# Eight subtractions moved from VectorE to GpSimd, and a small indirect transfer ahead of the first gathers, in a routed expert kernel

## The chip, the cores and the metric

The kernel runs on one core of one Trainium2 chip. The metric is device microseconds of one execution. Traces are of one profiled execution; times in them count from its first instruction. Engines are named as in the profile: PE is TensorE's matmuls and PEld its weight loads, DVE is VectorE, ACT is ScalarE, POOL is GpSimd, SP is SyncE.

## The reference

Windowed attention with a linear bias makes the tokens of a mixture of experts. Each expert takes exactly 4608 / 8 = 576 tokens, given out greedily by descending score.

```python
# attention: batch 8, heads 8, sequence 576, head size 64, window 128
scores = where(mask, q @ k.T / 8 + bias, -1e9)
x = (softmax(scores) @ v)            # -> tokens [4608, 512]

# experts: N, D, E, F = 4608, 512, 8, 1024
cap = N // E
logits = x @ w_gate
for idx in argsort(-logits.flatten()):      # greedy, each token once, each expert at most cap
    tok, e = idx // E, idx % E
    if assigned[tok] < 0 and counts[e] < cap:
        assigned[tok] = e; counts[e] += 1
for e in range(E):
    mask = assigned == e
    out[mask] = maximum(x[mask] @ w1[e], 0) @ w2[e]
```

All inputs and outputs are float32.

## The kernel before

**Two parts.** `attention` runs first (to about 203 us); it stores the tokens to `x`, a tensor in device memory, with DMAs on SP's queue. Then `Router.start` finds the tokens of the first expert (`phase(0)`, VectorE with small matmuls), and `layer_moe` does the experts one by one. The route of expert k+1 and k+2 (`phase`, a generator that is advanced from `slot`) is worked out by VectorE while TensorE multiplies for expert k.

**Exactness by two parts.** The matmuls take fp32r operands, so each operand is split into a high part (the value rounded to fp32r) and a low part (what is left). `MoE.split` does so for weights: from a raw float32 chunk of 128x1024 ScalarE makes the high part (line 896), and VectorE subtracts it from the raw chunk to get the low part, in two halves of 512 columns (line 898). Both lie in one tile `hl`. The raw tiles have 4 buffers (`raw`), the split ones 10 (`wt`). An expert has four chunks for its first layer and four for its second.

**An expert.** `gather` issues five indirect DMAs on POOL's queue (line 907), which fetch the expert's tokens by the indices `idx`. `turn` transposes them on TensorE and splits them into `xh` and `xl` (lines 931 to 935). `layer1` multiplies (line 954), ScalarE makes the high part of the result `hh` (line 960), VectorE the low one `hlo` (line 965). `layer2` multiplies high by high, high by low weights, low by high (lines 983, 984, 986), and the result goes out by an indirect DMA on POOL's queue (line 995). For expert 0 `layer1` does the first 256 tokens for all columns before the rest, and the last two of its five transposes come later.

**What sets the order.** Tiles and semaphores are laid out by a planner that runs through the program with a cost for each instruction and writes out a fixed order for each engine; an instruction that comes earlier in the program has priority when several are ready in the plan. `keep_in_program_order` and `issue_after` hold some instructions to the program's order. On the chip, each engine goes through its list in that order, and one that waits holds up all behind it on its engine. Where loads and splits stand in the program is set by two lists, of which each entry is expert (relative to k), layer, chunk and earliest slot:

```python
W_SPLIT = [(0, 1, 0, 2), (0, 1, 1, 6), (0, 1, 2, 10), (0, 1, 3, 14),
           (1, 0, 0, 17), (1, 0, 1, 20), (1, 0, 2, 23), (1, 0, 3, 26)]
```

The first four are the second layer of the current expert, the others the first layer of the next. The first layer of expert 0 is split in `layer_moe` itself.

**The route's steps on VectorE, and what waits for them.** For an expert after the first, `few` picks 16 candidates per partition (lines 791 to 807: `q`, `qt`, `few`, `fy`, `fq`, `fa`, `OHf`), then three times a key (`kf`, line 817), an indicator (`ind`, line 565) and a count on TensorE (`m`, line 589). After that come `T` (695), the chosen expert's number `ei` (710), `m` (713), a running sum `run` (715), `ex` (717) with a matmul (720), and the indices `idx` (756). POOL does three instructions of this (lines 768, 773, 774), of 128x288 float32. The weights of an expert are loaded by SP only when its number `ei` is there (`loads`, lines 886 and 889). For expert 0 the route's instructions stand under line 456.

Of the kernel before, what the change touches and what calls it, by code (L numbers as in the profile page):

```python
# [5 lines left out]
F32 = mybir.dt.float32  # L6
F32R = mybir.dt.float32r
BF = mybir.dt.bfloat16
I32 = mybir.dt.int32
AF = mybir.ActivationFunctionType  # L10
ALU = mybir.AluOpType
# [4 lines left out]
E, DM, F, N = 8, 512, 1024, 4608  # L16
# [861 lines left out]
class MoE:  # L878
# [10 lines left out]
            nc.sync.dma_start(raw, (self.w1d, self.w2d)[layer][bass.ds(v, 1), c].rearrange("o p f -> (o p) f"))  # L889
            yield raw  # L890

    def split(self, raw):

        nc = self.nc
        hl = self.p["wt"].tile([128, 2, 1024], F32R, name="hl")
        self.last = nc.scalar.copy(hl[:, 0, :], raw)  # L896
        for c in (0, 512):
            nc.vector.tensor_tensor(hl[:, 1, c:c + 512], raw[:, c:c + 512], hl[:, 0, c:c + 512].bitcast(F32), ALU.subtract)  # L898
        return hl

    def gather(self, idx):
        nc = self.nc
        gs = []
        for h in range(5):
            r = 128 if h < 4 else 64
            g = self.p["g"].tile([128, DM], F32, name="g")
            nc.gpsimd.indirect_dma_start(out=g[:r, :], out_offset=None, in_=self.x,  # L907
                                         in_offset=bass.IndirectOffsetOnAxis(ap=idx[:r, h:h + 1], axis=0))
            gs.append((g, r))
        return gs  # L910
# [134 lines left out]

def layer_moe(tc, P, C, r, x, w1, w2, out, exact):
    m = MoE(tc, P, C, x, w1, w2, out)
    g = m.gather(r.idx[0])
    raw = list(m.loads(r.ei[0], 0, range(SOON)))
    route = (n for k in range(1, E) for n in r.phase(k, exact))  # L1050
    with tc.issue_after(r.last.ins):
        for _ in range(EARLY0):
            next(route)
    W = {(0, 0): [m.split(raw[c]) for c in range(HI0)]}
    with tc.issue_after(r.last_pe.ins):
        m.idle = P["ps_h"].tile([128, 512], F32, name="ph")
        m.keep_warm(WARM0)
    tn = m.turn(g, True)
    with tc.issue_after(m.last.ins):
        next(tn)  # L1060

    with tc.issue_after(m.turned.ins):
        late = P["rt"].tile([1, 1], I32, name="late")
        last = tc.nc.vector.tensor_copy(late, r.ei[0][0:1, 0:1])
    raw += list(m.loads(late, 0, range(SOON, 4)))
    with tc.issue_after(m.last.ins):
        for _ in range(TURN0 - 1):
            next(tn)
    W[0, 0] += [m.split(raw[c]) for c in range(HI0, 4)]
    with tc.issue_after(last.ins):  # L1070
        for _ in range(EARLY - EARLY0):
            next(route)
    for _ in tn:
        pass
    st = dict(wait=0, turn=0)
    raws, loaders = {}, {}

    def slot(k, i):

        st["wait"] -= 1  # L1080
        if st["wait"] <= 0 and (k + 1 not in r.idx or k + 2 not in r.idx and i >= AHEAD[min(k, 2)]):
            st["wait"] = next(route, 0)
        for e, layer, c, due in W_LOAD:
            e += k
            if i >= due and e in r.ei and len(raws.get((e, layer), ())) == c:
                if c == 0:
                    loaders[e, layer] = m.loads(r.ei[e], layer)
                    raws[e, layer], W[e, layer] = [], []
                raws[e, layer].append(next(loaders[e, layer]))
                break  # L1090
        for e, layer, c, due in W_SPLIT:
            e += k
            if i >= due and len(W.get((e, layer), (0,) * 9)) == c and len(raws[e, layer]) > c:
                W[e, layer].append(m.split(raws[e, layer][c]))
                break
        if i >= 16 and k + 1 in r.idx:
            if k not in gathers:
                gathers[k], st["turn"] = m.turn(m.gather(r.idx[k + 1])), i + TURN_WAIT
            elif i >= st["turn"]:
                next(gathers[k], None)  # L1100
                st["turn"] = i + TURN_STEP

    gathers = {}
    for k in range(E):
        i = 0
        for _ in m.layer1(W.pop((k, 0)), m.xg, k == 0):
            slot(k, i)
            i += 1
        for _ in range(9):
            if len(W.get((k, 1), ())) < 4:  # L1110
                slot(k, i - 1)
        for _ in m.layer2(W.pop((k, 1)), m.h, r.idx[k], k == E - 1):
            slot(k, i)
            i += 1
        if k == E - 2:

            with tc.issue_after(m.sent.ins):
                m.nc.gpsimd.drain()
        if k < E - 1:
            while k + 1 not in r.idx:  # L1120
                next(route)
            while len(W.get((k + 1, 0), ())) < 4:
                slot(k, 31)
            if k not in gathers:
                gathers[k] = m.turn(m.gather(r.idx[k + 1]))
            for _ in gathers[k]:
                pass
# [12 lines left out]
def moe_attn_kernel(tc, qk, v, w1, w2, wn, rel, ident, cst, out):  # L1140
    nc = tc.nc
    with ExitStack() as es:
# [25 lines left out]
        for k, b in (("ps_g", 1), ("ps_h", 4), ("ps_o", 2)):  # L1168
            P[k] = es.enter_context(tc.tile_pool(name=k, bufs=b, space=PSUM))
        layer_moe(tc, P, C, r, x, w1, w2, out, False)  # L1170
        again = P["rs"].tile([1, 1], I32, name="again")
        nc.vector.tensor_copy(again, r.flag[0:1, 0:1])
        go = nc.values_load(again[0:1, 0:1], min_val=0, max_val=1)
        with tc.If(go > 0):
            r.start(True)
            layer_moe(tc, P, C, r, x, w1, w2, out, True)
# [26 lines left out]
```

## Time and profile before

| | |
|---|---|
| median of 3 runs | 692.58 us (692.04 to 695.5) |
| the profiled execution | 692.76 us, its span 691.0 us |
| mean granted TensorE clock | 0.983 |
| PE busy | 660.8 us (96%) |
| DVE busy | 453.4 us (66%) |
| ACT busy | 325.1 us (47%) |
| POOL busy | 152.4 us (22%) |
| low parts of weights on DVE (line 898) | 128 instructions, 682 ns each |
| gathers on POOL (line 907) | 40 instructions, 1086 ns each |

The span is from the first to the last instruction of the profiled execution; the execution's own time has a little around it. Busy time is the union of an engine's instructions; on POOL it is rough. In the order of time a row gives start and duration in us, engine, line, operation, output and inputs, shapes, count, and in brackets how long the engine stood idle before and what ended it.

### The profile page before, as it was taken

Reading aid. Unit: us, or ns where it says so; the run is one execution under the profiler, and the core shown is the slowest. Engines: PE = TensorE matmul, PEld = TensorE weight load, DVE = VectorE, ACT = ScalarE, POOL = GpSimd, SP = SyncE. Lnnn points to the kernel's source line nnn. Section 1 sums busy time; section 2 is a strip of 40 time slices with the busy share of each in tenths; the row PEclk is TensorE's granted clock in tenths of the full one; section 3 lists DMA queues with packets and bytes.
Section 4 is the critical chain, followed back from the end, with each engine's and each line's share of the span. In section 5 each row is a group of like instructions: output and inputs, shape, how many; then the busy total and the mean of one; then the engine's idle time right before and its main releaser. Section 6 shows DMA issues by size and latency. Waiting matters only on the chain.

```text
span 691.0 us, 18850 instructions
## 1 busy us (share of the span) xinstructions
PE 660.8 (96%) x7266; PEld 581.2 (84%) x7267; DVE 453.4 (66%) x1876; ACT 325.1 (47%) x991; POOL 152.4 (22%) x337
## 2 busy tenths in 40 slices
PE   8999999999973999899999999999999999999996
PEld 5899889989872788689789889889988988988986
DVE  6678888887877889699578738818846524523210
ACT  6898899898861434333243233224214324323211
POOL 4122222222120204113250231131132022011011
PEclk9999999999995999999999999999999999999999
DMA  8466665757332707335263245135135325301001
GB/s 313 139 205 206 195 227 173 219 179 223 109 90 80 228 25 251 121 131 191 74 206 102 93 132 158 45 123 183 55 114 172 104 92 152 110 30 39 1 25 49
DMA packets 35138, 92.71 MB, mean 134 GB/s; under 512 B 3808, under 2 KB 13152, under 8 KB 35040
## 3 DMA queue, kind: packets, MB, share of 16 engines
q1 hardware_dynamic: 29152, 72.55, 32.4%
q0 software_dynamic: 5888, 18.88, 8.4%
q8 instruction: 59, 0.97, 0.6%
q14 instruction: 39, 0.32, 0.2%
HBM read 72.54 MB, written 18.87 MB: 132 GB/s over the span
## 4 chain that ended last, share of the span: by engine, by line
PE 85%; DVE 7%; DMA 4%; ACT 2%; issue 1%; SPq 0%; POOL 0%; POOLq 0%; DVEq 0%
PE ph L954 26%; PE po L983 10%; PE po L984 10%; PE po L986 8%; PE s L53 7%; PE x L53 7%; PE pt L53 7%; PE pt L160 6%; PE pg L931 2%; DMA raw<-in_w_dram 2%; DVE hl L898 1%; ACT hl L896 1%; ACT u L147 1%; PE m L589 1%; DMA rel_sb<-in_rel_dram 1%
## 5 line engine op out<-in xcount | busy, mean ns | idle before, releaser
L954 PE MATMUL ph<-xh,hl 128*128 128x288 f32 (+2 forms) x1024 | 189.8, 299 | 0.0
L954 PEld LDWEIGHTS ph<-xh,hl 128*128 128x128 f32 x1024 | 154.3, 189 | 1.0
L983 PE MATMUL po<-hl,hh 128*128 128x512 f32 (+1 forms) x328 | 130.8, 399 | 0.0
L147 ACT ACTIVATE u<-u,mn 128x192 f32<-128x192 f32 (+2 forms) x288 | 124.0, 438 | 5.5 <-DVE mn L137 5.5
L984 PE MATMUL po<-hl,hh 128*128 128x512 f32 (+1 forms) x328 | 126.5, 386 | 0.0
L954 PE MATMUL ph<-xl,hl 128*128 128x288 f32 (+2 forms) x512 | 115.7, 298 | 0.0
L960 ACT ACTIVATE hh<-ph 128x288 fp32r<-128x288 f32 (+2 forms) x128 | 46.8, 408 | 144.6 <-PE ph L954 144.3
L986 PE MATMUL po<-hl,hlo 128*128 128x512 f32 (+1 forms) x264 | 102.1, 387 | 0.0
L898 DVE TENSOR_TENSOR hl<-raw,hl 128x512 fp32r<-128x512 f32 x128 | 84.9, 682 | 13.7 <-ACT hl L896 13.2
L137 DVE CUSTOM_DVE_ANT_0 u<-s,bm 128x192 f32<-128x192 f32 (+1 forms) x248 | 71.8, 346 | 32.4 <-PE s L53 31.7
L995 POOL DMA_INDIRECT out_dram<-o,idx x40 | 44.6, 1116 | 204.2 <-ACT o L990 125.0
L954 PEld LDWEIGHTS ph<-xl,hl 128*128 128x128 f32 x512 | 84.1, 189 | 0.1
L935 DVE TENSOR_TENSOR xl<-pg,xh 128x512 fp32r<-128x512 f32 (+1 forms) x37 | 23.7, 640 | 83.0 <-ACT xh L934 82.9
L965 DVE SCALAR_TENSOR_TENSOR hlo<-ph,hh 128x288 fp32r<-128x288 f32 (+2 forms) x128 | 49.8, 417 | 39.7 <-ACT hh L960 39.5
L896 ACT CAST hl<-raw 128x1024 fp32r<-128x1024 f32 x64 | 65.5, 1049 | 17.1 <-DMA raw<-in_w_dram 12.1
L983 PEld LDWEIGHTS po<-hl,hh 128*128 128x128 f32 x328 | 61.8, 188 | 11.1
L984 PEld LDWEIGHTS po<-hl,hh 128*128 128x128 f32 x328 | 61.9, 189 | 10.6
L990 ACT COPY o<-po 128x512 f32<-128x512 f32 (+1 forms) x33 | 18.9, 573 | 95.5 <-PE po L986 60.5
L907 POOL DMA_INDIRECT g<-x,idx x40 | 43.4, 1086 | 83.4 <-PE pg L931 33.8
L53 PE MATMUL s<-qk 64*64 64x192 f32 (+1 forms) x992 | 60.5, 327 | 0.6 <-DMA qk<-in_qk_dram 0.3
L986 PEld LDWEIGHTS po<-hl,hlo 128*128 128x128 f32 x264 | 49.6, 188 | 10.1
L147 ACT ACTIVATION_READ_ACCUMULATOR u<-u,mn 128x1 f32 x288 | 55.8, 194 | 0.0
(236 smaller groups left out, 939.2 us busy)
## 6 DMA issues: line engine op xcount, KB each, us to landing
raw<-in_w_dram SPq DMA_DIRECT2D x64, 512.0 KB, 4.3
qk<-in_qk_dram SPq DMA_DIRECT2D x32, 576.0 KB, 5.1
v<-in_v_dram SPq DMA_DIRECT2D x32, 288.0 KB, 3.8
x<-xb SPq DMA_DIRECT2D x14, 512.0 KB, 3.7
x<-xb SPq DMA_DIRECT2D x8, 128.0 KB, 3.4
x<-xb SPq DMA_DIRECT2D x4, 256.0 KB, 2.5
g<-x,idx POOLq DMA_INDIRECT x40, 3.4
out_dram<-o,idx POOLq DMA_INDIRECT x40, 2.8
```

The lines of the kernel that those rows point to most:

```text
L53: put(nc.tensor.matmul(out, w, a, start=start, stop=stop, skip_group_check=True))
L137: put(nc.vector.tensor_tensor_reduce(out=weights(n, t, h), in0=x[:, c:c + 64 * m].rearrange("q (j k) -> q j k", k=64), in1=bm[n % NP][:, y ...
L147: put(nc.scalar.activation(u, u, AF.Exp, bias=st["mn"][:, i:i + 1], scale=-1.0, accum_out=st["sm"][:, i:i + 1]))
L896: self.last = nc.scalar.copy(hl[:, 0, :], raw)
L898: nc.vector.tensor_tensor(hl[:, 1, c:c + 512], raw[:, c:c + 512], hl[:, 0, c:c + 512].bitcast(F32), ALU.subtract)
L954: nc.tensor.matmul(pp[t], w[:, a, j, fo:fo + 128], x[:, j, cut[t]:cut[t + 1]], start=(j == 0 and a == 0 and x is xh), stop=(j == 3 and a = ...
L960: nc.scalar.activation(o, pp[t], AF.Relu)
L965: nc.vector.scalar_tensor_tensor(d, pp[t][:, c0:c1], 0.0, o[:, c0:c1].bitcast(F32), ALU.max, ALU.subtract)
L983: nc.tensor.matmul(out, a, wh, start=(f == 0), stop=False)
L984: nc.tensor.matmul(out, a, wl, start=False, stop=(f == 7 and t == 4))
L986: nc.tensor.matmul(out, hl[:, f, 128 * t:128 * t + 128], wh, start=False, stop=(f == 7))
L995: self.sent = nc.gpsimd.indirect_dma_start(out=self.out, out_offset=bass.IndirectOffsetOnAxis(ap=idx[:r, t:t + 1], axis=0), in_=o[:r, :], ...
```

## The change

Two things are done.

`rehearse` is called at the start of `layer_moe`, before the first `gather`. On POOL it sets 16 indices to zero and issues one indirect DMA that fetches row 0 of `x` 16 times into 16 partitions of a tile of the output pool `o` (3 buffers); nothing reads it. As a read of `x` it waits for the stores of `x`.

`split` takes an engine for the subtraction. In `slot` that is GpSimd where the expert's number is 0. The only entries with that number are those of expert 0's second layer (the first four of `W_SPLIT` at k = 0): four chunks, two halves each, eight instructions of 128x512. All other splits stay on VectorE.

```diff
-    def split(self, raw):
+    def split(self, raw, eng=None):
 
         nc = self.nc
         hl = self.p["wt"].tile([128, 2, 1024], F32R, name="hl")
         self.last = nc.scalar.copy(hl[:, 0, :], raw)
         for c in (0, 512):
-            nc.vector.tensor_tensor(hl[:, 1, c:c + 512], raw[:, c:c + 512], hl[:, 0, c:c + 512].bitcast(F32), ALU.subtract)
+            (eng or nc.vector).tensor_tensor(hl[:, 1, c:c + 512], raw[:, c:c + 512], hl[:, 0, c:c + 512].bitcast(F32), ALU.subtract)
         return hl
+
+    def rehearse(self):
+
+        nc = self.nc
+        row = self.p["rt"].tile([16, 1], I32, name="row", bufs=1)
+        nc.gpsimd.memset(row, 0)
+        got = self.p["o"].tile([128, DM], F32, name="o")
+        nc.gpsimd.indirect_dma_start(out=got[:16, :], out_offset=None, in_=self.x,
+                                     in_offset=bass.IndirectOffsetOnAxis(ap=row[:, 0:1], axis=0))
...
     m = MoE(tc, P, C, x, w1, w2, out)
+    m.rehearse()
     g = m.gather(r.idx[0])
...
             if i >= due and len(W.get((e, layer), (0,) * 9)) == c and len(raws[e, layer]) > c:
-                W[e, layer].append(m.split(raws[e, layer][c]))
+                W[e, layer].append(m.split(raws[e, layer][c], None if e else m.nc.gpsimd))
                 break
```

## The prediction

> **What bounds the kernel now.** I read the page first, then the granted clock and busy time by stage, then TensorE's waits, and only then the order of time around each wait.
>
> ```profile
> span 691.0 us, 18850 instructions
> PE   8999999999973999899999999999999999999996
> ```
> ```profile
> 231.00:243.00 12.00, 12.00 (x101) 11.85 (x98) 10.43 (x41) 7.40 (x12) 0.00 (x0) 1.00 0.83 278
> 243.00:246.00 3.00, 1.63 (x20) 1.20 (x19) 2.13 (x7) 2.04 (x5) 0.00 (x0) 1.00 0.07 27
> 246.00:260.00 14.00, 13.87 (x98) 12.34 (x98) 12.21 (x56) 2.74 (x7) 1.91 (x3) 1.00 0.01 2
> 260.00:295.00 35.00, 32.91 (x200) 26.58 (x200) 27.29 (x97) 14.18 (x20) 10.36 (x9) 1.00 0.53 184
> 295.00:303.00 8.00, 7.10 (x54) 6.61 (x51) 7.13 (x32) 1.42 (x4) 3.15 (x4) 1.00 0.08 19
> ```
> ```profile
> PE m L589 <- DVE ind L565: 3.1, 2, 1.8
> PE m L720 <- DVE ex L717: 1.4, 2, 1.0
> PE pg L931 <- DMA g<-x,idx: 0.8, 1, 0.8
> ```
>
> The first fence is the page: TensorE is full in nearly every slice. The second is busy time by stage (columns after the length: PE, weight load, DVE, ACT, POOL, clock, DMA share, GB/s). The third is TensorE's waits from 222 us to the end. From there on it waits 3.1 + 1.4 + 0.8 = 5.3 us in all, five times, the last of them in the stage that ends at 303. So whatever this change can give without removing matmuls is at most 5.3 us. Four waits are for VectorE's routing of the next experts; one is for the first gather. The clock is full in all these stages, so it is not in the sum.
>
> The change's stage is 231 to 303 us. VectorE is busy 12.21 of 14 us from 246 to 260: while TensorE starts expert 0, VectorE both routes expert 1 and makes low parts.
>
> **Part 1, the small transfer ahead of the gathers.** It adds on POOL's queue one memset and one indirect DMA of 16 rows, both before the five gathers, and takes one buffer of the output tile, not used before expert 0's second layer.
>
> ```profile
> 206.53 0.47 SPq L273 DMA_DIRECT2D x<-xb  x1
> L907 POOLq EVENT_SEMAPHORE  x30: 17/17/14065, 206.4 to 565.0; - x30
> 222.73 0.33 DVE L456 SCALAR_TENSOR_TENSOR idx<-ia 64x5 int32<-64x5 f32 x2
> 224.03 1.18 POOL L907 DMA_INDIRECT g<-x,idx  x1 [22.18 <-DVE L L456]
> 225.52 1.13 POOL L907 DMA_INDIRECT g<-x,idx  x1 [0.30 <-issue]
> 227.59 0.66 PE L931 MATMUL pg<-ident_sb,g 128*128 128x128 f32 x4 [0.79 <-DMA g<-x,idx]
> 266.27 0.32 DVE L756 SCALAR_TENSOR_TENSOR idx<-ia 64x5 int32<-64x5 f32 x2
> 267.33 1.04 POOL L907 DMA_INDIRECT g<-x,idx  x1 [7.39 <-issue]
> ```
>
> Its own cost lies in a hole: it must wait for the last store of x (issued at 206.53 on SP, which it does not pass), and POOL's queue stands in one wait of 14.07 us until the indices come. A gather's issue takes 1.18 us, so the cover is some ten times what is put in it; without that cover it would cost its 1.2 us ahead of the gathers.
>
> What it can give: the first indices end at 223.06 and the first gather starts at 224.03, 0.97 us later. Against the second gather, which follows the first by 0.30, up to 0.67 of that could be a cold first issue. But expert 1's gather, no longer the first, starts 267.33 - 266.59 = 0.74 us after its indices. That is the nearest row (same form, same wait), so I take 0.97 - 0.74 = 0.2 us, with ends 0 and 0.67. Below nothing is excluded by the 14 us hole. TensorE's wait for this gather is 0.79 us, so no more than that could be had.
>
> **Part 2, eight subtractions from VectorE to POOL.** Four weight chunks of expert 0's second layer, two halves each (first row, with least, median and greatest ns, and first and last start):
>
> ```profile
> L898 DVE TENSOR_TENSOR hl<-raw,hl x8: 676/680/686, 240.0 to 249.4; 128x512 fp32r<-128x512 f32 x8
> L774 POOL TENSOR_TENSOR L<-Lt,L 128x288 f32<-128x288 f32 x6 | 5.1, 850 | 0.5
> L299 POOL TENSOR_TENSOR by<-Lp 128x160 f32<-128x160 f32 x7 | 3.7, 524 | 0.6
> 238.16 1.05 ACT L896 CAST hl<-raw 128x1024 fp32r<-128x1024 f32 x1
> 257.22 0.43 POOL L773 TENSOR_SCALAR Lt<-T 128x288 f32<-128x288 bf16 x1 [26.55 <-DVE T L695]
> 259.03 0.14 DVE L710 TENSOR_SCALAR ei<-ef 128x1 int32<-128x1 f32 x1
> 246.18 0.39 PE L984 MATMUL po<-hl,hh 128*128 128x512 f32 x1
> 246.41 0.39 PE L986 MATMUL po<-hl,hlo 128*128 128x512 f32 x1
> 264.12 0.40 PE L984 MATMUL po<-hl,hh 128*128 128x512 f32 x1
> ```
>
> VectorE loses 8 x 0.68 = 5.4 us. POOL's price is an estimate from its own two subtraction-like rows: (850 - 524) / (288 - 160) = 2.55 ns per column, so 850 + 224 x 2.55 = 1.42 us for 512 columns, 11.4 us for eight. POOL is idle 26.55 us before 257.22, so it has room. The first cast ends at 239.21, so uninterrupted POOL would be done near 251. Two things must hold to call this free on TensorE. The first low part used (246.18) needs only chunk 0, ready near 242. The next one is used at 264.12; its cover is 13 us. And the raw buffers, which POOL frees up to 2 us later than VectorE did, are next loaded for expert 1, whose number comes at 259.03. Without these covers the price would be POOL's lateness one for one.
>
> Now what VectorE's relief is worth at each TensorE wait. First the wait of 1.37 us:
>
> ```profile
> 239.98 0.68 DVE L898 TENSOR_TENSOR hl<-raw,hl 128x512 fp32r<-128x512 f32 x1
> 240.69 0.68 DVE L898 TENSOR_TENSOR hl<-raw,hl 128x512 fp32r<-128x512 f32 x1
> 241.28 0.17 DVE L802 TENSOR_SCALAR fy<-few 128x16 f32<-128x16 f32 x1
> 242.10 0.17 DVE L805 SCALAR_TENSOR_TENSOR fa<-fq,few 128x16 bf16<-128x16 f32 x1
> 242.26 0.69 DVE L898 TENSOR_TENSOR hl<-raw,hl 128x512 fp32r<-128x512 f32 x1
> 242.86 0.22 DVE L807 TENSOR_TENSOR OHf<-c_eb,fa 128x128 bf16<-128x128 bf16 x1
> 243.90 0.68 DVE L565 TENSOR_TENSOR ind<-kf,c_i 128x1024 bf16<-128x1024 bf16 x1
> 244.63 0.42 PE L589 MATMUL m<-OHf,ind 128*128 128x16 bf16 x8 [1.37 <-DVE ind L565]
> ```
>
> Three of the eight stand ahead of `ind` in VectorE's order, each holding back the next instruction by 0.60 (240.69 to 241.28, for one): 1.8 us, more than the wait. So the upper end is all 1.37. The lower end is set by what happens when POOL and VectorE read at once:
>
> ```profile
> L713 DVE SCALAR_TENSOR_TENSOR m<-am,kmx,sel x7: 236/561/564, 258.5 to 530.6; 128x36 bf16<-128x36 bf16 x7
> L715 DVE TENSOR_TENSOR_SCAN run<-c_ones,m x7: 215/851/859, 259.4 to 531.1; 128x36 bf16<-128x36 bf16 x7
> 258.54 0.56 DVE L713 SCALAR_TENSOR_TENSOR m<-am,kmx,sel 128x36 bf16<-128x36 bf16 x1
> 258.39 0.67 POOL L768 TENSOR_TENSOR L<-L,pen 128x288 f32<-128x288 f32 x1 [0.74 <-DVE ov L776]
> ```
>
> `m` takes 0.24 us alone and 0.56 as a rule; here it ends at 259.10, just after POOL's subtraction ends at 259.06. `run` takes 0.22 alone and 0.85 as a rule. So a VectorE instruction with two inputs in SBUF stands until POOL's running one is done: 0.32 and 0.64 us, 50 to 75% of a POOL instruction. [...]
>
> Ahead of the wait there are three such: `fa`, `OHf` and `ind`. If POOL runs its 1.42 us instructions back to back from 239.21, they end near 240.65, 242.1, 243.5; each of the three VectorE instructions slips in after one of them, `ind` starts near 243.6 to 244.0, and 0 to 0.3 of the 1.37 is won. The measured rows are nearer to that end than to a free run, but only if POOL is always ahead, so I take 0.4, ends -0.1 and 1.37.
>
> The second long wait, 1.78 us:
>
> ```profile
> 282.23 0.42 PE L589 MATMUL m<-OHf,ind 128*128 128x16 bf16 x8 [1.78 <-DVE ind L565]
> ```
>
> It is the first count of expert 2's routing, and stands behind expert 1's. After `ind` at 243.90 five of the eight are left (they end by 250), 5 x 0.60 = 3.0 us off VectorE's queue, less one more `ind` that may meet POOL (at most 1.42). So expert 1's routing can run some 1.6 to 3.0 us earlier, as far as TensorE's count matmuls, which stand between layer matmuls at places the planner chose, move with it. Those places are not seen here. Ends 0 and 1.78; I take 0.7, under half, since both the planner and expert 1's weight transfers stand between. The two waits for `ex` (1.4 together) come from `m` and `run` meeting POOL's older instructions, which stay: 0.1, ends 0 and 1.4.
>
> **Sum.** 0.2 + 0.4 + 0.7 + 0.1 = 1.4 us. The profiled execution took 692.76 us (span 691.0 and 1.76 around it), so 691.4 by it, with a span of 689.6. The median of the runs is 692.58, 0.18 below; from there 691.2, which is my number.
>
> **Rivals.**
> (a) All of VectorE's waits go: POOL's subtractions fall mostly between VectorE's two-input instructions, and the planner moves the counts forward. Then 0.67 + 1.37 + 1.78 + 1.4 = 5.2 us: 687.4. For it: VectorE is the only thing these waits name. Against it: `m` and `run` met POOL in nearly all of seven executions.
> (b) The exclusion eats it: the 4 two-input instructions from 240 to 251 (`fa`, `OHf`, two `ind`) each stand a whole 1.42, 5.7 us, against 8 x 0.60 = 4.8 won. VectorE gains nothing or loses 0.9, and the time is 692.6 to 693.5, no change. For it: the same seven rows. Against it: a full wait each time needs the worst phase.
> (c) Slower: TensorE comes to wait for POOL. No POOL row writes fp32r, the type of the low part, so 1.42 us is from another output type. In the order seen, each of the eight may take (264.12 - 239.21) / 8 = 3.1 us before anything waits; that is the point from which it decides. At three times my price, 4.26 us, POOL ends at 239.21 + 34.1 = 273.3, while the last low part is wanted about 18 matmuls of 0.23 us (246.18 to 246.41) after 264.12, at 268.3. TensorE stands 5.0 us there, and the time is 692.58 + 5.0 - 0.2 = 697.4. Against it: VectorE's 0.68 us for this form is no more than 512 columns cost it with another type (`ind`, 1024 columns of bf16, 0.68), so the type need not matter. Fillers such as the matmul at 246.18, drawn forward onto a low part not yet made, would cost less.
> (d) The small transfer does nothing: then 0.2 is missing, inside the range; it is part of every case.
>
> **How the numbers follow.** Partial gain as summed 0.46, (a) 0.22, (b) 0.22, (c) 0.10. Within 0.5% (3.46 us, about what a measurement of this kernel can tell from no change) lie the forecast and (b): 0.68. (a) is faster and (c) slower by over that. The range runs from (a), 687.4, to 694.5, 1.0 beyond (b)'s 693.5 for fillers that wait a little on POOL; the forecast's own part of it is 689.1 to 692.6.
>
> **What would show it.** Expert 0's eight POOL subtractions near 1.4 us each, back to back from 239 to 252. `ind` before 243.9, and TensorE's first wait for it well below 1.37; that at 282 below 1.78. `fa`, `OHf` or `ind` longer than 0.17, 0.22 and 0.68 would show the exclusion. The first gather 0.74 us after its indices, not 0.97. Wrong would be: TensorE waiting for a low part on POOL, a POOL price far from 1.42, or a layer order so changed that new waits appear after 303.

## The result and the profile after

The changed kernel takes 700.56 us (median of 6 runs, 699.31 to 700.98) against 692.31 us before (6 runs beside it): slower, ratio 1.011 with a 95% interval of 1.0089 to 1.0131. The prediction was 691.2 us, in a range of 687.4 to 694.5, with 0.10 for slower. It was wrong in sign and far outside its range.

The page of the changed kernel, span and two rows of the 40 slices (PE busy, granted TensorE clock):

```profile
span 698.7 us, 18859 instructions
PE   8999999999965799899999999999999999999995
PEclk9999999999985979999999999999999999999999
```

The fourteenth slice of TensorE (227 to 244.5 us) has gone from 9 to 7, and in the fifteenth the clock row has a 7. (The 6 and 5 ahead of it are the route of expert 0, which was there before; the slices are wider now.) TensorE's waits from 222 us on (us in total, times, longest):

```profile
PE m L589 <- DVE ind L565: 7.0, 2, 5.4
PE m L720 <- DVE ex L717: 1.4, 2, 0.9
PE pg L940 <- DVE xl L944: 0.9, 1, 0.9
```

Three of the five waits of before are as they were: the second one for `ind` is 1.56 us (1.78), the two for `ex` are 0.43 and 0.94 (0.44 and 0.96). The one for the first gather (0.79) is gone. The first one for `ind` has grown from 1.37 to 5.41 us, and a wait of 0.92 us for `xl` is new. VectorE's own time line shows where the 5.41 us come from (start, length):

```profile
239.08 0.19 DVE L798 MAX8 few<-qt 128x8 f32<-128x36 f32 x1
239.30 0.17 DVE L802 TENSOR_SCALAR fy<-few 128x16 f32<-128x16 f32 x1
239.51 1.20 DVE L803 TENSOR_SCALAR fq<-fy 128x16 f32<-128x16 f32 x1
240.74 1.19 DVE L805 SCALAR_TENSOR_TENSOR fa<-fq,few 128x16 bf16<-128x16 f32 x1
241.85 0.16 DVE L812 TENSOR_SCALAR fy<-fq 128x16 f32<-128x16 f32 x1
241.96 1.25 DVE L807 TENSOR_TENSOR OHf<-c_eb,fa 128x128 bf16<-128x128 bf16 x1
243.14 1.25 DVE L817 TENSOR_SCALAR kf<-fy 128x32 bf16<-128x32 f32 x1
244.43 1.69 DVE L565 TENSOR_TENSOR ind<-kf,c_i 128x1024 bf16<-128x1024 bf16 x1
```

And POOL in the same stretch, six subtractions in a row and then two, and the same by tile (least, median and greatest ns):

```profile
238.13 7.45 POOL L898 TENSOR_TENSOR hl<-raw,hl 128x512 fp32r<-128x512 f32 x6 [8.80 <-ACT hl L896]
249.58 2.52 POOL L898 TENSOR_TENSOR hl<-raw,hl 128x512 fp32r<-128x512 f32 x2 [4.01 <-ACT hl L896]
```
```profile
L898 POOL TENSOR_TENSOR hl<-raw,hl x8: 1259/1281/1295, 238.1 to 250.8; 128x512 fp32r<-128x512 f32 x8
```

Of VectorE's six instructions from `fq` on, five last some 1.0 us longer than they need (0.17 to 0.69 us, shown with the fourth experiment), one POOL subtraction each: the two engines take turns, one for one, through the whole chain that ends in `ind`. Only one `fy` slipped through in a gap. Not every VectorE instruction is held: `few`, with one input, took its own 0.19 us at 239.08, while POOL's first subtraction (238.13 to 239.42) was running. The rest of the loss is in the granted clock (busy time by stage; after the stretch and its length come PE, PEld, DVE, ACT and POOL with their counts, then the clock, DMA share and GB/s):

```profile
231.00:240.80 9.80, 9.78 (x80) 9.42 (x78) 8.65 (x32) 6.04 (x10) 2.67 (x3) 1.00 0.92 291
240.80:246.30 5.50, 0.12 (x4) 0.12 (x5) 5.47 (x6) 1.33 (x2) 4.78 (x4) 0.68 0.14 57
246.30:253.00 6.70, 6.70 (x35) 5.92 (x35) 5.12 (x15) 2.28 (x4) 2.52 (x2) 0.50 0.00 0
253.00:262.00 9.00, 9.00 (x73) 8.28 (x71) 6.72 (x38) 1.75 (x4) 1.53 (x3) 1.00 0.01 2
```

TensorE stands from 240.8 to 246.2, and when it goes on it runs at clock 0.50 until 253.1: 35 matmuls in the 6.7 us of the third row, where the 9 us after it hold 73. In TensorE's time line the same matmuls are, first before the hole and then behind it:

```profile
239.06 0.28 PE L963 MATMUL ph<-xl,hl 128*128 128x256 f32 x1
239.18 0.40 PE L963 MATMUL ph<-xh,hl 128*128 128x256 f32 x2
239.42 0.28 PE L963 MATMUL ph<-xl,hl 128*128 128x256 f32 x1
...
249.09 0.41 PE L963 MATMUL ph<-xl,hl 128*128 128x256 f32 x1
249.30 0.63 PE L963 MATMUL ph<-xh,hl 128*128 128x256 f32 x2
249.73 0.41 PE L963 MATMUL ph<-xl,hl 128*128 128x256 f32 x1
```

Three matmuls of 256 columns take 0.36 us from start to start (239.06 to 239.42), then 0.64 (249.09 to 249.73). So 6.9 us at half clock do the work of 6.9 x 0.36 / 0.64 = 3.9, and 3.0 us are lost.

**Where the profiled 7.76 us went** (span 690.98 to 698.74). Measured from the first matmul of expert 0's first layer: to the first of expert 1's, 63.90 us before and 71.59 after, +7.69. From there to the last matmul nothing (390.12 and 390.09). Ahead of it the profiled run of before lost 1.29 in the attention, to a stretch of half clock (3.41 us from 22.93) that after's doesn't have; behind it, after's last scatter took 1.39 longer (7.33 against 5.94 us from the last matmul to the end). That last piece is 6.0 to 6.9 us in six of the kernels below and 7.6 to 8.0 in four, with no visible relation to the edit, so it is not counted as an effect of the change. The +7.69 is +4.73 of TensorE standing (5.41 - 1.37, 0.92, less 0.23 at the others) and 2.96 in the rest, which is what the spacing gave for the half clock.

### The profile page after: what moved, and what is told of

It is laid out like the page before. It is cut to its first block, busy times and chain, and to the rows that moved or that the text cites. A ratio compares the mean times of both kernels' runs of the same rounds, so it can differ in the third digit from the quotient of the medians.

```text
span 698.7 us, 18859 instructions
## 1 busy us (share of the span) xinstructions
PE 662.3 (95%) x7266; PEld 582.7 (83%) x7267; DVE 456.4 (65%) x1868; ACT 325.6 (47%) x991; POOL 162.4 (23%) x347
## 4 chain that ended last, share of the span: by engine, by line
PE 84%; DVE 8%; DMA 3%; ACT 2%; issue 1%; SPq 0%; POOL 0%; POOLq 0%; DVEq 0%; ACTq 0%
PE ph L963 26%; PE po L992 10%; PE po L993 10%; PE po L995 8%; PE s L53 7%; PE x L53 7%; PE pt L53 6%; PE pt L160 6%; PE pg L940 2%; DMA raw<-in_w_dram 2%; DVE hl L898 1%; ACT hl L896 1%; PE ph L924 1%; ACT u L147 1%; PE m L589 1%
## 5 line engine op out<-in xcount | busy, mean ns | idle before, releaser
L898 DVE TENSOR_TENSOR hl<-raw,hl 128x512 fp32r<-128x512 f32 x120 | 79.3, 684 | 15.0 <-ACT hl L896 14.7
L999 ACT COPY o<-po 128x512 f32<-128x512 f32 (+1 forms) x33 | 18.9, 574 | 95.8 <-PE po L995 60.8
L995 PEld LDWEIGHTS po<-hl,hlo 128*128 128x128 f32 x264 | 49.7, 188 | 10.2
```

Of the source, the lines that this page charges most:

```text
L898: (eng or nc.vector).tensor_tensor(hl[:, 1, c:c + 512], raw[:, c:c + 512], hl[:, 0, c:c + 512].bitcast(F32), ALU.subtract)
L995: nc.tensor.matmul(out, hl[:, f, 128 * t:128 * t + 128], wh, start=False, stop=(f == 7))
```

## The experiments

The theory: VectorE's instructions stand until POOL's running subtraction is done ("exclusion", as in the prediction's rival (b); `m` 0.56 us against 0.24 in before); the half clock follows from TensorE's hole. Rivals: the small transfer; the planner's order, which changed with the edit; POOL's total work or lateness. In the changed kernel VectorE's order up to `ind` is that of before less three subtractions, except that two `hlo` which stood ahead of `ind` now stand behind it. On TensorE 86 layer-1 matmuls stand ahead of the first count, where before has 96.

### 1. The small transfer alone

```diff
-                W[e, layer].append(m.split(raws[e, layer][c], None if e else m.nc.gpsimd))
+                W[e, layer].append(m.split(raws[e, layer][c]))
```

> The small transfer stays, all subtractions go back to VectorE. Exclusion theory (VectorE's instructions stand behind POOL's subtractions, five of them ahead of `ind`): as before, 691.5 to 693.5 us, TensorE's first wait for `ind` near 1.4 us. Rival 1 (the small transfer is the cause): 698 or more. Open in both: the time from the last matmul to the end, 5.9 us before and 7.3 after; if the small transfer makes it, it shows here.

692.46 us, ratio 0.9991 (0.9972 to 1.0009): as before. The first wait for `ind` is 0.69 us, less than expected, and the end takes 6.90 us from the last matmul. The small transfer isn't the cause.

It isn't worth anything either. The first gather starts 0.87 us after its indices are there, here and in the changed kernel, and 0.97 us in before and in kernels 2 to 4 below, which don't have it: 0.10 us. TensorE's wait for the gather is gone, but what stands in its place is the kernel's 15 matmuls of zeros ahead of the first transposes, which run at half clock until 225.3 us:

```profile
221.30 5.39 PE L924 MATMUL ph<-zero 128*128 128x512 bf16 x15 [0.22 <-issue]
226.66 0.66 PE L940 MATMUL pg<-ident_sb,g 128*128 128x128 f32 x4
```

From the first of these to the first transpose it is 5.36 us here, 5.53 in the changed kernel, and 5.09 in before with its 0.79 us of waiting. The half clock ends at 225.8 in the changed kernel and at 224.3 in before. So where the wait is gone it is because the zeros took longer, not because the gather came sooner.

### 2. The subtractions alone

The transfer is left out (`m.rehearse()` is taken away), the rest is the changed kernel.

> The eight subtractions on POOL, without the small transfer. Exclusion theory: as the changed kernel, 699 to 701 us, first wait for `ind` 5.0 to 5.6 us, `fq`, `fa`, `OHf`, `kf` 1.2 us each and `ind` 1.7. Rival 1: as before, 692 to 693.

700.83 us, ratio 1.0100 (1.0077 to 1.0123), and its first wait is 5.67 us:

```profile
PE m L589 <- DVE ind L565: 7.3, 2, 5.7
```

In its time line `fq` takes 1.22, `fa` 1.19, `OHf` 1.35, `kf` 1.25 us; here `fy` was caught too (1.30), and `ind` was not (0.69). The whole loss is in the subtractions.

### 3. The same work on POOL in shorter instructions

```diff
-        for c in (0, 512):
+        n = 256 if eng else 512
+        for c in range(0, 1024, n):
```

> As the run with POOL alone, but each 512-column subtraction is made as two of 256 columns (some 0.65 to 0.7 us each). The work on POOL is the same. Exclusion theory: each VectorE instruction stands half as long, so five times 0.5 instead of five times 1.05: first wait for `ind` 2.5 to 3.0 us, little half clock after it, 694 to 697 us. Rival 2 (the planner's order or POOL's total work is the cause, not the length of one instruction): wait near 5 us, 699 to 701.

698.69 us, ratio 1.0079 (1.0050 to 1.0108). The first wait is 2.74 us, half of 5.67, though POOL is busy as long as before or longer (16 instructions of 733 ns in the median, against 8 of 1281):

```profile
L899 POOL TENSOR_TENSOR hl<-raw,hl x16: 719/733/1172, 238.2 to 249.1; 128x256 fp32r<-128x256 f32 x16
```
```profile
239.67 0.65 DVE L803 TENSOR_SCALAR fq<-fy 128x16 f32<-128x16 f32 x1
240.36 0.66 DVE L805 SCALAR_TENSOR_TENSOR fa<-fq,few 128x16 bf16<-128x16 f32 x1
...
241.05 0.71 DVE L807 TENSOR_TENSOR OHf<-c_eb,fa 128x128 bf16<-128x128 bf16 x1
241.69 0.72 DVE L817 TENSOR_SCALAR kf<-fy 128x32 bf16<-128x32 f32 x1
242.44 1.15 DVE L565 TENSOR_TENSOR ind<-kf,c_i 128x1024 bf16<-128x1024 bf16 x1
```

Each VectorE instruction stands some 0.5 us, half as long. So it is the length of one POOL instruction that counts, times the number of VectorE's instructions in the chain, and not POOL's work. The time was expected at 694 to 697; it came out higher: a wait of 2.74 us still brought 6.8 us of half clock (6.4 of them with TensorE at work), and the transposes of expert 1 waited 1.44 us for `xl`.

### 4. The same order, with POOL silent

```diff
+            if eng:
+                eng.memset(hl[:, 1, c:c + 512].bitcast(F32), 0.0)
+                continue
```

> POOL writes zeros where the low parts stand, and reads nothing; the low parts of expert 0's second layer are left out. VectorE's order up to `ind` is that of the changed kernel. Exclusion theory, if it takes POOL's reads: `fq`, `fa`, `OHf`, `kf` and `ind` take their own 0.17 to 0.68 us, the first wait for `ind` is below 1 us, 688.5 to 692 us. If POOL's writes alone block too: wait 2 to 5 us. Rival 2 (the order of the instructions): wait near 5 us, about 700.

693.01 us, ratio 1.0001 (0.9984 to 1.0019). The memsets wait for nothing, so POOL made them from 229.1 to 232.9 us, and it is idle while the chain runs:

```profile
239.25 0.18 DVE L803 TENSOR_SCALAR fq<-fy 128x16 f32<-128x16 f32 x1
239.46 0.17 DVE L805 SCALAR_TENSOR_TENSOR fa<-fq,few 128x16 bf16<-128x16 f32 x1
239.55 0.17 DVE L812 TENSOR_SCALAR fy<-fq 128x16 f32<-128x16 f32 x1
239.67 0.22 DVE L807 TENSOR_TENSOR OHf<-c_eb,fa 128x128 bf16<-128x128 bf16 x1
239.81 0.17 DVE L817 TENSOR_SCALAR kf<-fy 128x32 bf16<-128x32 f32 x1
240.02 0.69 DVE L565 TENSOR_TENSOR ind<-kf,c_i 128x1024 bf16<-128x1024 bf16 x1
```

These are the instructions of the changed kernel in the same order, at their own lengths. `ind` ends at 240.71, in the changed kernel at 246.12; the five delays there, 1.20 - 0.18, 1.19 - 0.17, 1.25 - 0.22, 1.25 - 0.17 and 1.69 - 0.69, make 5.1 of these 5.4 us. TensorE's first wait is 0.34 us. So the planner's order doesn't make the long wait. It does move the count: counted from its first layer-1 matmul, TensorE comes to it after 11.04 us in this order, as in the changed kernel, and after 12.24 in before. Even so the wait falls from 1.37 to 0.34 with POOL silent, and the 5.07 from there to 5.41 are the holding. Kernel 7 below has the same order up to `ind`, with all its low parts, and no first wait.

The wait for `xl` belongs to the order and not to the holding: 0.78 us of it stands here too. What makes it was not followed further. Whether POOL's writes alone would hold VectorE this run says only in passing: `OH`, with two inputs in SBUF, ran at 229.32, among the memsets, in 0.30 us, as in the second kernel where POOL did nothing then.

And yet it isn't faster than before (688.5 to 692 was expected), though it has the first wait almost gone. That is a question of its own (7 to 9).

### 5. POOL with one input

```diff
+            if eng:
+                eng.tensor_copy(hl[:, 1, c:c + 512], raw[:, c:c + 512])
+                continue
```

> POOL copies the raw chunk into the low part (one input read, the same writes) in place of subtracting, without the small transfer; the low parts of expert 0's second layer are wrong values. If any SBUF read by POOL shuts VectorE out: `fq`, `fa`, `OHf`, `kf` and `ind` stand as long as one POOL copy (wait 2 to 5.5 us, by its length), 694 to 700. If only a POOL instruction with two inputs does: own lengths, wait below 1 us, 690 to 693 as with the writes alone.

694.44 us, ratio 1.0029 (1.0013 to 1.0045); the first wait is 1.88 us in the profiled execution (698.32 us, the slowest of ten). `fq` and `fa` are held, each to the end of a copy of 0.61 us that had begun some 0.1 us ahead of it, and the rest falls where POOL has no copy:

```profile
240.82 0.55 DVE L803 TENSOR_SCALAR fq<-fy 128x16 f32<-128x16 f32 x1
241.41 0.52 DVE L805 SCALAR_TENSOR_TENSOR fa<-fq,few 128x16 bf16<-128x16 f32 x1
241.85 0.16 DVE L812 TENSOR_SCALAR fy<-fq 128x16 f32<-128x16 f32 x1
241.96 0.22 DVE L807 TENSOR_TENSOR OHf<-c_eb,fa 128x128 bf16<-128x128 bf16 x1
```

So these copies, POOL instructions with a single input, held VectorE as well: by 0.37 and 0.35 us, some 60% of the copy.

### 6. Filling TensorE's hole

Matmuls of zeros that wait for `fa` alone, just ahead of the first count, to keep the clock up: 16 of them, and then 8.

```diff
         cnt = self.bank()
+        for _ in range(fill):
+            self.tc.keep_in_program_order(self.nc.tensor.matmul(cnt[0:16, :], fa, self.C["zero"], start=True, stop=True))
```

> The changed kernel, with 16 matmuls of zeros (each 512 columns, into the count's own PSUM bank, overwritten by the count) put just ahead of TensorE's first count, waiting for `fa` alone: TensorE has work from about 241.9 us on instead of standing until 246.2. The count itself can't start earlier. Clock theory (of the 7.7 us lost between the first and the last matmul of the experts, some 3 us are TensorE at half clock after its 5.4 us of standing): the granted clock stays at 1.0 from 246 to 253, the time is 697 to 698.5 us. Rival (the rest of the loss comes from the order of the later work, not from the clock): 700 to 701.5 as the changed kernel.

> The changed kernel with 8 matmuls of zeros ahead of the first count in place of 16; with 16 they ran at half clock, ended 1.2 us after `ind` and held the count up. Eight take 2.6 us at half clock from 242.1 us and end before `ind`. Clock theory: clock 1.0 from about 246.3 us on, the first count at 246.2 as in the changed kernel, and the 96th layer-1 matmul 18.0 to 19.5 us after the first instead of 21.1; the time 697 to 698.5 us. Rival (the half clock costs nothing that isn't lost elsewhere): 700 to 701 us.

700.85 us, ratio 1.0114 (1.0093 to 1.0134), and 700.74, ratio 1.0112 (1.0087 to 1.0137): no gain, so both expectations of the time failed. The clock did what was expected with 16:

```profile
239.90:246.30 6.40, 4.19 (x12) 1.47 (x13) 6.33 (x7) 2.09 (x2) 6.40 (x6) 0.73 0.23 83
246.30:253.00 6.70, 6.70 (x61) 5.39 (x59) 4.25 (x19) 1.63 (x4) 2.33 (x2) 1.00 0.00 0
```

From 246.3 to 253.0 TensorE does 61 matmuls at clock 1.00 where the changed kernel does 35 at 0.50. But the zeros themselves ran at half clock from 242.9 to 246.3 and ended 1.2 us after `ind`, the planner moved layer matmuls, and the later waits grew by 1.5 us together, with another 3.4 us of half clock at 287. With 8, one more VectorE instruction met POOL: `ind` ended at 247.7, TensorE stood another 1.89 us, and a second stretch of half clock came at 249.1. So the filling is no clean test of what the half clock costs; that price rests on the spacing above and on the table below.

### 7 to 9. The relief on VectorE itself

What the change was to bring can be had without POOL: expert 0's low parts stay on VectorE, but are issued after the first `ind` (kernel 7). Kernels 8 and 9 shift expert 1's first transposes by 2 and 3 slots as well.

```diff
+                with tc.issue_after(first.ins) if e == 0 and not exact else ExitStack():
-                W[e, layer].append(m.split(raws[e, layer][c]))
+                    W[e, layer].append(m.split(raws[e, layer][c]))
...
-                gathers[k], st["turn"] = m.turn(m.gather(r.idx[k + 1])), i + TURN_WAIT
+                gathers[k], st["turn"] = m.turn(m.gather(r.idx[k + 1])), i + TURN_WAIT + (0 if k else 2)
```

> The kernel before (subtractions on VectorE, no small transfer), but expert 0's second-layer low parts are issued after the first `ind`, so the three subtractions that stood ahead of it stand behind it. Exclusion theory: nothing shuts VectorE out, `ind` ends 1 to 2 us earlier, the first wait is below 0.5 us instead of 1.4, 690.5 to 692.5 us; that is the relief which the change was after, without POOL. If this also gives nothing, VectorE's own queue was not what the first wait was worth.

> The kernel in which expert 0's second-layer low parts are made on VectorE after the first `ind`, and expert 1's first transposes stand two slots (11 matmuls in TensorE's order, some 2.6 us) later, since TensorE stood 4.30 us there for the gather. If what that kernel won at the first count (2.0 us by the 96th layer-1 matmul) was given back at this gather alone: the wait is 1.5 to 2 us, no half clock after it, 690 to 692 us. If the loss only moves on (to the second count or to the next expert's weights): 694 to 695.5 us as without the shift.

> The same with three slots (20 matmuls, some 4.8 us): the gather's wait is gone, 688.5 to 691 us by the first account; 694 to 695.5 by the second. Transposes that end too late for expert 1's first layer would show as a wait of `ph` near 295 us.

694.85 us, ratio 1.0043 (1.0026 to 1.0060); 692.19 us, 0.9987 (0.9966 to 1.0009); 693.29 us, 1.0004 (0.9987 to 1.0021). In 7 `ind` ends at 240.62 and the first wait is gone, and so is the second, but a new one stands at the gather of expert 1:

```profile
PE pg L931 <- DMA g<-x,idx: 5.3, 2, 4.3
PE m L720 <- DVE ex L717: 1.7, 2, 1.0
```

In the planner's new order TensorE comes to the first transposes at 269.88, and they start at 274.18, when the gather has landed. Two slots later the wait is 1.97 us, three slots later 0.53, but then the second count waits 2.00. That wins back what 7 lost, and no more. The clock takes its part again, in kernel 8 right behind its 1.97 us:

```profile
274.50:277.90 3.40, 3.40 (x10) 2.87 (x11) 1.61 (x5) 1.53 (x2) 1.94 (x2) 0.50 1.00 381
277.90:295.00 17.10, 17.10 (x103) 13.03 (x102) 11.67 (x44) 5.30 (x8) 2.93 (x3) 1.00 0.23 83
```

None of the versions beats the kernel before by more than can be measured. Kernel 7 missed its 690.5 to 692.5 us; 8 came 0.2 us above its 690 to 692, with a half clock that was not expected; 9 fell between its two ranges.

### All kernels in one account

From the first matmul of expert 0's first layer to the first of expert 1's, each of these kernels makes the same 192 matmuls of the first layer and 112 of the second, and the same transposes and counts (the two with zeros are left out). Worked out from each trace: length of this stretch, TensorE's gaps in it, what is left, and the time at half clock while TensorE was working.

| kernel | length us | gaps us | left us | half clock us |
|---|---|---|---|---|
| before | 63.90 | 3.58 | 60.32 | 0 |
| 1 transfer alone | 63.76 | 2.96 | 60.80 | 0 |
| 4 POOL silent | 65.16 | 3.12 | 62.04 | 3.4 |
| 7 later on VectorE | 67.09 | 5.06 | 62.03 | 3.4 |
| 8, turn + 2 | 65.03 | 2.78 | 62.25 | 3.4 |
| 9, turn + 3 | 65.73 | 3.39 | 62.34 | 3.4 |
| 3 shorter POOL instructions | 69.25 | 6.21 | 63.04 | 6.4 |
| 5 POOL copies | 68.76 | 5.21 | 63.55 | 6.8 |
| changed | 71.59 | 8.31 | 63.28 | 6.9 |
| 2 POOL alone | 72.39 | 9.01 | 63.38 | 7.2 |

What is left grows with the half clock: 60.3 to 60.8 without any, 62.0 to 62.3 with 3.4 us, 63.0 to 63.6 with 6.4 to 7.2. Each us at half clock goes with about 0.4 more (0.39 by a straight line through the ten), a little under the 0.44 of the spacing (1 - 0.36 / 0.64). And it says why the relief brings nothing in kernel 8's profiled execution: 0.8 us less of gaps than before, and 1.9 paid in clock. Each row is one execution, and this one took 694.31 us, against a median of 692.19.

It is not the length of a gap alone that decides whether half clock follows: 1.97 and 2.00 us in kernels 8 and 9 brought it; 1.78 in before, 1.77 in kernel 1 and 2.20 (at 285.4) in the kernel with 8 zeros did not. The last section shows what separates them.

## Why the prediction was wrong, point by point

**The step that failed** is in the first wait: "Ahead of the wait there are three such: `fa`, `OHf` and `ind`." That such instructions, with two inputs in SBUF, are held it had from `m` and `run` (0.56 us against 0.24, and 0.85 against 0.22). That those with one input are not held was its assumption; no row that it gives shows this. In the changed kernel `fq` and `kf`, with one input each, took 1.20 and 1.25 us instead of 0.18 and 0.17. Five instructions were held, not three.

**The price of one** was put at "50 to 75% of a POOL instruction", from `m` and `run`, which had met POOL instructions that were already under way. In a chain against back-to-back POOL work each VectorE instruction arrives just after the next POOL one has begun: 1.00 to 1.08 us of 1.28, some 80% (with the shorter instructions of kernels 3 and 5 some 0.5 of 0.73 and 0.36 of 0.61). So "slips in after one of them" was right for when they run, and wrong for how many POOL instructions this lasts. `ind` was put at 243.6 to 244.0, in the times of before. It came at 244.43 in an execution whose first layer-1 matmul is 1.30 us earlier (229.73 against 231.03), so at 245.7 in the times of before, and was itself held for 1.0.

**The place of the count** was taken as fixed for this wait. In the new order TensorE comes to it 1.2 us earlier (11.04 us after its first layer-1 matmul, not 12.24), so part of the relief was used up by the plan. By the kernel with POOL silent the relief was worth 1.03 us of the wait, and the holding cost 5.07: the term of 0.4 us gained, with a lower end of -0.1, measured -4.04.

**Rival (b)** was this mechanism, with "VectorE gains nothing or loses 0.9" as its outcome. It set 4 instructions against the 4.8 us that VectorE is relieved of. But only three of the eight subtractions stood ahead of `ind`, 1.8 us of relief, against 5.1 us of holding in the same place; the relief behind `ind` was no use there. It also took "a full wait each time" for the worst phase, while the two engines, which took turns here, kept this phase through five instructions (1.00 to 1.08 us of 1.28 each).

**"The clock is full in all these stages, so it is not in the sum"** left out 3.0 us. It was true of before, and the change of the waits made it untrue. Without it the result would still have been slower, by 4.7 us in that stretch.

**The small transfer**, 0.2 us, measured 0.10 at the gather and nothing at the end, since the 15 matmuls of zeros, longer by their half clock (5.69 us, 4.30 in before), stood in the place of the wait. **The second wait**, 0.7, measured 0.22; **the waits for `ex`**, 0.1, measured 0.03. Against them the `xl` wait of 0.92 was not seen.

**Right** were POOL's part: 1.28 us per subtraction where 1.42 was estimated; TensorE never waited for a low part, so rival (c), the only one on the slower side, had the right sign for a reason that didn't occur, so its 0.10 is no credit to the mechanism; with its fp32r output the subtraction was no dearer than estimated from rows with f32 output. The sign named for the exclusion, `fa`, `OHf` or `ind` longer than 0.17, 0.22 and 0.68, is what the trace showed first.

## What to carry to other kernels

Before moving an elementwise instruction to GpSimd, look at what VectorE runs in the same microseconds: if that is a chain of short instructions of the kinds held here (`fa`, `OHf` and `ind` with two inputs in SBUF, `fq` and `kf` as `tensor_scalar` of 16 and 32 columns: 1.00 to 1.08 us longer each) that someone waits for, the price is the number of links times most of the length of one GpSimd instruction (60 to 80% here), not the work moved. If it must go there, cut it into short instructions (0.73 us in place of 1.28 brought the wait from 5.67 to 2.74) or place it where VectorE has no such chain (not tried here). And a wait of TensorE that grows can cost more than itself (behind the 5.41 us here came 6.9 at half clock, 3.0 of them lost): count what the clock takes behind it, and compare versions by gaps and half clock separately.

## What the runs showed of the hardware beyond that

Half clock came in stretches of 3.4, 6.8 and 10.2 us here (and of 17.1 and 20.5 around the route of expert 0, in before from 207.25 and in the changed kernel from 205.28), multiples of one length, and within each trace the stretches also begin whole multiples of 3.413 us apart: in the changed kernel at 205.28, 242.82 and 696.80, which are 11 and 144 steps behind the first. So each trace can be cut into windows of 3.41 us on its own grid, and the twelve traces have 2345 of them that begin in the program at full clock. Where TensorE was busy for at most 1.53 us of a window, half clock followed in all 35 cases; with more than 1.98 us, in none of 2295; in between, in 2 of 15. So a window need not be empty for half clock to follow: that at 239.41 in the changed kernel had 1.37 us of work. The gap of 1.97 us in kernel 8 lay in one window, which was left with 1.44. The 2.20 us in the kernel with 8 zeros were cut by an edge at 286.6, and the two windows kept 2.15 and 2.48. The 1.78 us in before lay in one window that kept 1.63, in the band where it goes either way: kernel 4 was caught there with 1.95, the changed kernel not with 1.85, and why stays open, as does how many windows a stretch lasts.

The grid has no fixed place in the program: its first edge is at 0.48 us in the changed kernel and at 2.45 in before. So the same gap may be paid for in one execution and not in the next. The runs are in keeping with that, without showing it window by window: the twelve executions of kernel 8 have granted clocks of 0.979 to 0.986 and take 690.62 to 696.46 us.
